# Transposing row tiles two matmuls earlier, and moving one projection between the last value products

## The chip, the cores and the metric

The kernel runs on one core of one Trainium2 chip. The metric is the device time of one execution in microseconds, taken as the median of several. A profiled execution gives a trace with a start and a recorded end for every instruction. In the views of the profile PE is the tensor engine, PEld its weight loads, DVE VectorE, ACT ScalarE, POOL GpSimd and SP SyncE; a q behind a name marks the start of a transfer on that engine's queue, and L302 is line 302 of the kernel.

## The reference

```python
def reference(A_x, A_k_cache, A_v_cache, A_wq, A_wo, B_x, B_w_gate, B_w_up, B_w_down):
    x = A_x                                   # (1, 2048, 640)
    xn = _layernorm(x, axis=-1)
    s = _A_ref(xn, A_k_cache, A_v_cache, A_wq, A_wo)   # attention, 32 heads of 192, last 512 keys
    g = _silu(_B_ref(xn, B_w_gate, B_w_up, B_w_down))  # (sigmoid(xn@Wg) * (xn@Wu)) @ Wd
    return x + s * g
```

All arrays are bfloat16. There is no causal mask: every row meets the same 512 keys.

## The kernel before

Two places matter. In the **prologue** the first 512 rows are taken as four row tiles of 128. A tile is centred on VectorE (tile 0 in part on ScalarE), turned on the tensor engine by five transposes (`turn_pe`), copied by ScalarE in two parts out of PSUM (the memory that the matmuls write), and then serves as weights for five gate and five up matmuls of 512 columns (`tile_half`, with half 0 for gate and 1 for up; `c0`, `c1` choose some of the five chunks).

```python
        def turn_pe(t, c0=0, c1=NCD, k=3):
            pT = bank[k][:, t % 2, 0:NCD * H2].bitcast(BF16).rearrange("p (c n) -> p c n", c=NCD)
            for c in range(c0, c1):
                nc.tensor.transpose(pT[:, c, :], xn_t[t][:, c * P:(c + 1) * P], ident[:])
            for d0, d1 in ((c0, c1),) if c1 - c0 < NCD else ((0, 3), (3, NCD)):
                nc.scalar.activation(xcT[:, d0:d1, t * P:(t + 1) * P], pT[:, d0:d1, :], AF.Copy)
        ...
        for t in range(1, TQ):
            if t > 1:
                tile_half(t, 0, t % 3, 0)
            tile_half(t, 0, t % 3, 1, 0, 3)
            if t + 1 < TQ:
                turn_pe(t + 1)
            tile_half(t, 0, t % 3, 1, 3)
            if t == 1:
                tile_gated(0, 0, 0)
            tile_gated(t, 0, t % 3)
```

At the **end**, `values` (one head's product with V) and `project` (one row tile through Wo) run as two half passes each, which add into the same PSUM bank. Between the halves VectorE copies two numbers per partition out of the bank into `seen`. Only then may the second half start, so the copy is a marker that the first half is complete. `flow` puts other passes between the halves:

```python
    def values(u, h, k):
        ...
        for turn in range(2):
            ...                                # 16 matmuls of 193 columns, in pairs of 64 rows
            if turn == 0:
                nc.vector.tensor_copy(seen[:, DJ, :], bank[k][:, :, 0])
                yield
        ...                                    # reciprocal, then o_st = o4 * rden, both on VectorE

    def flow(jobs):                            # a0 b0 a1 c0 b1 d0 c1 ... : halves 0 and 1
        before = None
        for j in jobs:
            next(j)
            if before is not None:
                next(before)
            before = j
        next(before)

    order = (2, 3, 0, 1)
    ...
    flow([values(u + 1, h, order[h]) for h in range(4)]
         + [project(u - 1, 0, order[0], nc.scalar, nc.gpsimd)])
    for q in range(1, 4):
        next(project(u - 1, q, order[q], nc.scalar, nc.gpsimd, False))
    for q in range(4):
        next(project(u, q, order[q], nc.sync, nc.vector, False))
    last_rows()
```

The softmax here doesn't subtract the row's maximum and nothing guards it: scores larger than these inputs give would overflow.

## Time and profile before

| | before |
|---|---|
| median of the first three runs | 922.3 us |
| span of the profiled run (that run's time) | 919.8 us (921.55 us) |
| tensor engine busy | 99% of the span |
| last up matmul of tile 1 to first gate matmul of tile 2, start to start | 0.530 us (0.216 where nothing waits) |
| the same, tile 2 to tile 3 | 0.530 us |
| last score matmul to first 128-row projection ("the end stretch") | 8.139 us |

A matmul's recorded end is modelled (a 512-column matmul is recorded with 0.38 us and the next starts after 0.216), so distances between starts are what to read. Of the matmuls with gate, up and down weights and the first queries about one in fifty is missing from the trace (19 of 924); where one is, a distance looks twice as long and a count is one short.

### The profile page before, as it was taken

How to read it: one execution, taken by the hardware profiler on the slowest of the kernel's cores; microseconds unless marked ns; L12 is line 12 of the kernel's file. 1: busy time of each engine (PE TensorE's matmuls, PEld its weight loads, DVE VectorE, ACT ScalarE, POOL GpSimd, SP SyncE). 2: the span in 40 equal slices, each digit the busy share in tenths (PEclk: the TensorE clock that was granted, in tenths of full speed). 3: DMA queues.
4: the chain of work that ended last, by engine and by line, in shares of the span. 5: the costliest groups of instructions: out<-in, count | busy, mean ns of one | idle time of the engine just before them, and what ended most of it. 6: DMA issues, size and time to landing. Idle time of an engine off the chain costs nothing.

```text
span 919.8 us, 24974 instructions
## 1 busy us (share of the span) xinstructions
PE 913.4 (99%) x11314; PEld 622.9 (68%) x11333; DVE 492.9 (54%) x987; ACT 303.1 (33%) x334; POOL 126.7 (14%) x147
## 2 busy tenths in 40 slices
PE   9999999999999999999999999999999999999998
PEld 4445455466868686867676777777776767686885
DVE  6452522444646464646555555545564646464667
ACT  4222222255142424242333333242424151515150
POOL 2000100011002000200020011001100111055813
PEclk9999999999999999999999999999999999999999
DMA  9820330115434434342425162525251615246435
GB/s 319 165 44 1 89 87 1 43 62 88 80 61 110 83 59 81 94 98 44 97 83 109 36 105 79 113 32 108 65 110 44 113 61 88 62 96 142 89 72 138
DMA packets 173642, 79.35 MB, mean 86 GB/s; under 512 B 149952, under 2 KB 169616, under 8 KB 173536
## 3 DMA queue, kind: packets, MB, share of 16 engines
q1 hardware_dynamic: 166944, 58.47, 32.1%
q0 software_dynamic: 5040, 17.89, 6.7%
q8 instruction: 88, 1.44, 0.7%
q10 hardware_dynamic: 1552, 1.39, 0.5%
q14 instruction: 18, 0.15, 0.1%
HBM read 39.45 MB, written 2.62 MB: 46 GB/s over the span
## 4 chain that ended last, share of the span: by engine, by line
PE 99%; DMA 0%; DVE 0%; issue 0%; ACT 0%; DVEq 0%
PE bank L530 22%; PE bank L456 21%; PE bank L478 19%; PE bank L438 18%; PE bank L260 8%; PE bank L272 6%; PE bank L302 3%; PE bank L404 1%; DMA wg_sb<-in_B_w_gate_dram 0%; PE bank L563 0%; DVE o_sb L508 0%; DVE gate L513 0%; ACT xnT L246 0%; PE bank L244 0%; DVEq L665 0%
## 5 line engine op out<-in xcount | busy, mean ns | idle before, releaser
L442 ACT ACTIVATE E<-bank 128x1024 bf16<-128x1024 f32 x256 | 255.4, 1022 | 456.4 <-PE bank L438 456.3
L456 PE MATMUL bank<-xnT,wq_sb 64*128 64x512 bf16 x1800 | 226.4, 376 | 0.0
L530 PE MATMUL bank<-wo_sb,oT 64*128 64x320 bf16 x2688 | 205.2, 296 | 0.0
L438 PE MATMUL bank<-qT,kT 64*128 64x512 bf16 x1536 | 200.7, 376 | 0.0
L478 PE MATMUL bank<-vbuf,E 64*128 64x193 bf16 x4096 | 195.3, 243 | 0.0
L478 PEld LDWEIGHTS <-E 64*128 64x128 bf16 x4096 | 178.8, 94 | 10.2 <-issue 0.3
L530 PEld LDWEIGHTS <-oT 64*128 64x128 bf16 (+1 forms) x2892 | 163.3, 94 | 30.6 <-issue 0.3
L463 DVE CAST qT<-bank 128x1024 bf16<-128x1024 f32 x90 | 110.2, 1225 | 128.5 <-PE bank L456 128.5
L456 PEld LDWEIGHTS <-wq_sb 64*128 64x128 bf16 x1800 | 106.1, 100 | 87.0 <-issue 0.4
L438 PEld LDWEIGHTS <-kT 64*128 64x128 bf16 x1536 | 88.1, 94 | 73.5
L491 DVE TENSOR_TENSOR o_st<-bank,rden 128x768 bf16<-128x768 f32 x128 | 122.5, 957 | 4.4
L545 DVE TENSOR_TENSOR acc<-bank,acc 128x640 f32<-128x640 f32 x96 | 79.1, 824 | 20.1 <-PE bank L530 20.1
L118 POOL DMA_DIRECT2D vbuf<-in_A_v_cache_dram x28 | 21.1, 755 | 310.2 <-PE bank L478 307.3
L461 DVE COPY seen<-bank 128x2 f32<-128x2 f32 x90 | 14.3, 159 | 79.1 <-PE bank L456 79.1
L490 DVE RECIPROCAL rden<-bank 128x4 f32<-128x4 f32 x128 | 23.4, 183 | 60.6 <-PE bank L478 59.5
L272 PE MATMUL bank<-wd_sb,hT 128*128 128x128 bf16 (+1 forms) x377 | 52.4, 298 | 0.4
L272 PEld LDWEIGHTS <-hT 128*128 128x128 bf16 x384 | 29.7, 98 | 23.1
L260 PE MATMUL bank<-xnT,wu_sb 128*128 128x512 bf16 x177 | 44.6, 379 | 0.2
L260 PE MATMUL bank<-xnT,wg_sb 128*128 128x512 bf16 x176 | 44.5, 379 | 0.2
L266 DVE TENSOR_TENSOR hT<-bank,sig 128x512 bf16<-128x512 f32 x36 | 24.8, 690 | 37.1 <-ACT sig L263 37.1
L263 ACT ACTIVATE sig<-bank 128x512 bf16<-128x512 f32 x36 | 21.5, 597 | 55.8 <-PE bank L260 52.7
L110 POOL COPY k_perm<-k_st 128x768 bf16<-128x768 bf16 x32 | 25.5, 827 | 76.6 <-DMA k_st<-in_A_k_cache_dram 76.6
(52 smaller groups left out, 379.5 us busy)
## 6 DMA issues: line engine op xcount, KB each, us to landing
wo_sb<-in_A_wo_dram SPq DMA_DIRECT2D x7, 960.0 KB, 5.6
wq_sb<-in_A_wq_dram POOLq DMA_DIRECT2D x7, 960.0 KB, 6.0
k_st<-in_A_k_cache_dram POOLq DMA_DIRECT2D x14, 384.0 KB, 5.9
vbuf<-in_A_v_cache_dram POOLq DMA_DIRECT2D x28, 192.0 KB, 3.8
row<-in_A_x_dram SPq DMA_DIRECT2D x16, 160.0 KB, 2.4
oT<-o_st SPq DMA_TRANSPOSE x128, 3.2
x_sb<-in_A_x_dram SPq DMA_DIRECT2D x3, 640.0 KB, 9.5
wd_sb<-in_B_w_down_dram SPq DMA_DIRECT2D x1, 1920.0 KB, 13.8
```

The lines of the kernel that those rows point to most:

```text
L110: nc.gpsimd.tensor_copy(kp[:, pr, :, :, i * H2:(i + 1) * H2], kst[:, i, :, :].rearrange("p c (i j) -> p c j i", j=DJ),)
L260: nc.tensor.matmul(bank[k][:, half, 0:r1 - r0], lhsT=w[:, c, f * P:(f + 1) * P], rhs=xnT[:, b, c, r0:r1], start=(c == 0), stop=(c == NCD - 1))
L272: nc.tensor.matmul(wide(k)[:, d0:d1], lhsT=hT[b][:, f, q * P:(q + 1) * P], rhs=wd_sb[:, f, d0:d1], start=(f == 0), stop=(f == NF - 1))
L302: nc.tensor.matmul(bank[k][:, half, :], lhsT=xcT[:, c, t * P:(t + 1) * P], rhs=w[:, c, fg * FT:(fg + 1) * FT], start=(c == 0), stop=(c == ...
L438: nc.tensor.matmul(bank[k][:, i, :], lhsT=kT[r, pr, j, c * P:(c + 1) * P], rhs=q[r, pr * DJ + j, :], start=(j == 0), stop=(j == DJ - 1))
L442: nc.scalar.activation(E[u, pr][:, c, :, :], bank[k][:], AF.Exp, scale=scale_qk)
L456: nc.tensor.matmul(bank[k][:, half, :], lhsT=wq[r, c, col:col + DJ * (P - 1) + 1:DJ], rhs=xnT[r, b, c, :], start=(c == 0 and not second), ...
L463: nc.vector.tensor_copy(qT[u][:, 2 * m:2 * m + 2, :], bank[k][:])
L478: nc.tensor.matmul(o4[:, q, 0:DH + 1], lhsT=e[r, c, h % 2, q * P:(q + 1) * P], rhs=vbuf[r, h, c, 0:DH + 1], start=(turn == 0 and qq == 0 a ...
L491: nc.vector.tensor_tensor(o_st[u][:, :, h * DH:(h + 1) * DH], o4[:, :, 0:DH], rden[:].to_broadcast([P, TQ, DH]), ALU.mult)
L530: nc.tensor.matmul(res[:, half, :], lhsT=oT[u][r, cc, q * P:(q + 1) * P], rhs=wo[r, cc, half * HD:(half + 1) * HD], start=(turn == 0 and c ...
L545: nc.vector.tensor_tensor(cols(acc[:, t, :]), res, cols(acc[:, t, :]), ALU.add)
```

## The change

Its intent is to take away standing time of the tensor engine: in the prologue by putting four up matmuls instead of two behind the transposes, so that ScalarE's copy is done when the gate matmuls need it; at the end by putting a longer pass between the halves of the first value product.

```diff
-            tile_half(t, 0, t % 3, 1, 0, 3)
+            tile_half(t, 0, t % 3, 1, 0, 1)
             if t + 1 < TQ:
                 turn_pe(t + 1)
-            tile_half(t, 0, t % 3, 1, 3)
+            tile_half(t, 0, t % 3, 1, 1)
@@
-    flow([values(u + 1, h, order[h]) for h in range(4)]
-         + [project(u - 1, 0, order[0], nc.scalar, nc.gpsimd)])
+    flow([values(u + 1, 0, 2), project(u - 1, 0, 3, nc.scalar, nc.gpsimd),
+          values(u + 1, 1, 0), values(u + 1, 2, 1), values(u + 1, 3, 2)])
```

## The prediction

> **What bounds the kernel now.** I read the page first. Its span, 919.8 us, is of the profiled execution; the timed median is 922.3 us, 2.5 us more, and I carry that difference over unchanged.
>
> ```profile
> PE 913.4 (99%) x11314; PEld 622.9 (68%) x11333; DVE 492.9 (54%) x987; ACT 303.1 (33%) x334; POOL 126.7 (14%) x147
> ...
> PE 99%; DMA 0%; DVE 0%; issue 0%; ACT 0%; DVEq 0%
> ```
>
> The tensor engine is busy 99% of the span and is 99% of the chain of waits that ended last. The change moves instructions and removes none, so it can win only time in which the tensor engine stood still. I therefore looked next for such time in the view of waits, and then in the timeline of the two stretches that the diff touches. In the table of waits almost nothing lasts on this engine: its weight loads wait for ScalarE's copies into xnT five times, 2.0 us in total, all in the prologue.
>
> A matmul's end is modelled, so I count from start to start. In steady stretches five 512-column matmuls start every 1.08 us (13.64, then 14.73, then 15.81), which is 0.216 us each. The timeline of the prologue, with start and length in us, then shows this:
>
> ```profile
> 8.98 0.52 DVE L233 TENSOR_SCALAR xn<-x_sb,mv 128x384 bf16<-128x384 bf16 x2
> ...
> 9.86 0.44 PE L244 MATMUL bank<-ident,xn 128*128 128x128 bf16 x5
> ...
> 10.33 0.76 ACT L246 ACTIVATE xnT<-bank 128x384 bf16<-128x384 bf16 x2 [2.86 <-PE bank L244]
> 10.35 0.38 PE L302 MATMUL bank<-wu_sb,xnT 128*128 128x512 bf16 x1
> ...
> 10.88 1.25 PE L302 MATMUL bank<-wg_sb,xnT 128*128 128x512 bf16 x5 [0.15 <-ACT xnT L246]
> ...
> 12.62 0.44 PE L244 MATMUL bank<-ident,xn 128*128 128x128 bf16 x5
> 12.89 0.59 PE L302 MATMUL bank<-wu_sb,xnT 128*128 128x512 bf16 x2
> 13.10 0.77 ACT L246 ACTIVATE xnT<-bank 128x384 bf16<-128x384 bf16 x2 [0.84 <-PE bank L244]
> ...
> 13.64 1.25 PE L302 MATMUL bank<-wg_sb,xnT 128*128 128x512 bf16 x5 [0.15 <-ACT xnT L246]
> ```
>
> The last up matmul of tile 1 starts at 10.35. The next, the first gate matmul of tile 2, could start at 10.35 + 0.216 = 10.566, but starts at 10.88: 0.314 us are lost, twice the 0.15 that the view prints, because that counts from the modelled end. The cause is a chain: five transposes, ScalarE copies them out (first copy 10.33 to 10.825), and only then does the gate matmul have its weights. Only two up matmuls, 0.43 us, lie behind the transposes to cover about 0.75 us. The same happens for tile 3, whose last up matmul starts at 13.11: 13.64 - 13.327 = 0.314.
>
> The timeline of the end:
>
> ```profile
> 889.92 5.69 PE L478 MATMUL bank<-vbuf,E 64*128 64x193 bf16 x128
> ...
> 891.02 0.96 DVE L491 TENSOR_TENSOR o_st<-bank,rden 128x768 bf16<-128x768 f32 x1
> 891.89 0.46 DVE L485 COPY seen<-bank 128x2 f32<-128x2 f32 x2
> ...
> 895.43 0.99 PE L530 MATMUL bank<-wo_last,oT 64*128 64x320 bf16 x12
> ...
> 896.24 0.85 PE L478 MATMUL bank<-vbuf,E 64*128 64x193 bf16 x16
> 896.74 0.15 DVE L536 COPY seen<-bank 128x2 f32<-128x2 f32 x1
> 896.83 0.77 PEld L530 LDWEIGHTS <-oT 64*128 64x128 bf16 x12
> 896.94 12.51 PE L530 MATMUL bank<-wo_last,oT 64*128 64x320 bf16 x96
> ```
>
> In the chain view a value product (32 matmuls) takes 1.33 us and a projection (24) 1.63 us, so a half pass is 0.667 or 0.815 us. The eight value passes from 889.92 should end at 895.25, but the projection starts at 895.43: 0.18 us lost. It lies at 891.92, where the second half of the first value product waits for VectorE's small "seen" copy (891.89 to 892.04), which stands behind the 0.96 us eviction of the unit before. A second loss, 0.03 us, is at 896.94: 896.24 + 0.667 is 896.91, but the projection's second half waits for its own seen copy, which ends at 896.89.
>
> **What the Trainium skill says.** "TensorE: Matmul & The Clock Gate", section "Back-to-back issue gap", gives an isolated gap of N/2.4 + 2.5 ns: 216 ns for 512 columns and 136 for 320. The trace agrees (0.216; 1.63 us for 12 row-group pairs is 0.136). "Perfetto Trace Analysis", section "Tensor Engine Instruction (MATMUL, LD_WEIGHTS)", says that a matmul's profiled end is estimated from its size; this trace agrees, as matmuls of 0.38 us start 0.216 apart, so I use starts alone. "TensorEngine Tiling (Array Packing)", section "Key Properties", says that changing the tiling mode drains the engine. The trace has one such change near the edit: from 64-row to 128-row matmuls the next start is at 897.86 where 896.94 + 0.815 = 897.75 was due, 0.11 us. The change keeps this switch, behind another product.
>
> **Part one, the prologue.** The transposes of tiles 2 and 3 now stand behind one up matmul in place of three. No instruction is added. Four up matmuls, 0.864 us, then cover the copy. Worked out for tile 2: the transposes start two matmuls earlier, at 9.86 - 0.43 = 9.42; the copy keeps its distance of 0.48 us and starts at 9.90, and its first part (0.49 us) ends at 10.39; a release took 0.055 us before (10.825 to 10.88), so the gate matmul is free at 10.45 and due at 10.566. Slack 0.12 us, wait gone, 0.314 us won, and another 0.009 us because the first matmul behind the old wait took 0.225 us to the next. For tile 3 everything stands 0.32 us earlier as well: transposes at 11.86, copy 12.34 to 12.83 (ScalarE's two sigmoids also move up and end near 11.8), gate free at 12.89 and due at 13.005. Another 0.32 us. **Sum: 0.65 us won.**
>
> The earlier transposes need VectorE's centred rows sooner. For tile 2 the two parts end near 9.30 and 9.50; transpose 1 is due at 9.42 and transpose 4 at 9.59. Each part has its own wait in the built program, so with the same 0.055 us release the slack is 0.06 and 0.04 us: just enough. Tile 3's rows are ready at 11.15, well before 11.86.
>
> **Part two, the end.** The first half of one projection moves between the first two value products. Pass by pass, from the first value half at 890.585: the projection's half is due at 891.25, where its bank is free (the last exponential ends at 891.16, as before); it ends at 892.07, and the next value half is released at 892.10 by the same seen copy. The loss falls from 0.18 to 0.03 us. But now the fourth value product closes the sequence, with one pass (0.667 us) between its halves where it had two. Its seen copy stands in VectorE's order behind the second product's eviction. That product's second half runs 894.91 to 895.58; its reciprocal starts at 895.80 (0.22 us behind, as before), its eviction 896.02 to 896.98, the seen copy 896.89 to 897.04 (such copies start 0.08 us before the eviction's recorded end), and the matmul is released at 897.09. It was due at 896.91. A new wait of 0.18 us. Totals: before 0.18 + 0.03 = 0.21, after 0.03 + 0.18 = 0.21. **Sum: nothing**, within about 0.1.
>
> The early output row (VectorE, GpSimd, DMA) leaves about 3.8 us sooner, but it isn't the last row. The last unit's transposes wait for a free oT buffer until the other three projections have read theirs, near 902.9, so a later last eviction (near 899.4 in place of 898.3) doesn't delay them.
>
> **The total.** 922.3 - 0.65 + 0.0 = 921.65, say 921.7 us, 0.07% less.
>
> **Rivals.** First, the wait moves from ScalarE to VectorE: with 0.04 us of slack, a row of x that lands 0.3 us later than in this trace (DMA is saturated there, at some 350 GB/s) would cost up to 0.26 us of part one. For it: the first ten microseconds hang on transfers. Against it: the three times lie within 0.4 us of each other. Time: 921.9 or 922.0. Second, the tensor engine, now 0.65 us early, meets weights or transposed rows that have not landed, and gives the gain back: 922.3. Against it: no later wait of this engine for a DMA is in the list; in the trace the up weights next needed (at 16.24) land at 12.7, and the transposed rows needed at about 32.6 land at 30.5. Third, the new wait at the end is bigger than 0.18 us, because one more VectorE instruction slips in front of the seen copy: each 0.1 us there is 0.1 us of time, so 921.9 at 0.4 us. Or it doesn't arise and the end also wins its 0.18 us: 921.5.
>
> **Range and chances.** The removable standing time in both places is 0.63 + 0.21 us, so below about 921.4 there is nothing to be had except scatter; the repeats differ by up to 0.4 us. If most of part one is lost and the end loses 0.2, it is 922.4. I take 921.2 to 922.4. Two per cent is 18 us, over twenty times all that moves, so faster and slower get half a per cent each.
>
> **What would show it.** In the changed kernel's timeline the first gate matmul of tiles 2 and 3 should start 0.216 us behind the last up matmul, near 10.57 and 13.0, and the table of waits should lose these two waits for ScalarE. The transposes' loads should start without waiting for xn. At the end the value half behind the projection's half should wait 0.03 us or less, and the very last value half about 0.2 us. I would be wrong if the gate matmuls still wait, if a wait for xn over 0.1 us appears in front of the transposes, or if the last value half starts at once or waits over 0.4 us.

## The result, and the profile after

The changed kernel took 921.28 us in the median (921.04 to 921.51, four runs), the kernel before 922.2 us over four runs. The ratio is 0.9991 with a 95% interval of 0.9973 to 1.0008, so the times alone do not tell the two apart. A ratio here is the mean time of one kernel's runs over that of the other's of the same rounds, so not quite the ratio of the medians quoted.

The page of the changed kernel has the same picture as before, with 0.6 us less busy tensor engine:

```profile
PE 912.8 (99%) x11314; PEld 622.7 (68%) x11333; DVE 492.5 (54%) x987; ACT 303.3 (33%) x334; POOL 126.7 (14%) x147
```

The number drops although no matmul was removed: where nothing waits, the recorded matmuls overlap, so the first part of a wait behind one of them is counted as busy. Of the 0.62 us, 0.35 lie in the prologue between the first up matmul and the next rows' first gate matmul, where the two waits were; the other 0.27 lie before that, in the start-up, which differs from run to run (below). The view of waits, in us in total, number and longest, of the kernel before:

```profile
PEld L302 <- ACT xnT L246: 2.0, 5, 0.6
```

and of the changed kernel:

```profile
PEld L302 <- ACT xnT L246: 1.2, 5, 0.4
```

The group still counts five waits, but two of them are now weight loads that start ahead of time and hold nothing up. In the same view the waits of the matmuls themselves, `PE bank L302 <- ACT xnT L246`, go from two of 0.15 us to a single one of 0.28 us, at 5.46 in the start-up. That the loads are ahead of time is to be seen only in the timeline of the changed kernel's prologue (start, length, engine):

```profile
9.53 0.44 PE L244 MATMUL bank<-ident,xn 128*128 128x128 bf16 x5
...
9.81 1.03 PE L302 MATMUL bank<-wu_sb,xnT 128*128 128x512 bf16 x3
10.01 0.77 ACT L246 ACTIVATE xnT<-bank 128x384 bf16<-128x384 bf16 x2 [2.43 <-PE bank L244]
...
10.55 1.08 PEld L302 LDWEIGHTS <-xnT 128*128 128x128 bf16 x6 [0.21 <-ACT xnT L246]
...
10.67 1.24 PE L302 MATMUL bank<-wg_sb,xnT 128*128 128x512 bf16 x5
...
12.25 1.03 PE L302 MATMUL bank<-wu_sb,xnT 128*128 128x512 bf16 x4
...
12.99 1.30 PEld L302 LDWEIGHTS <-xnT 128*128 128x128 bf16 x7 [0.21 <-ACT xnT L246]
13.11 1.24 PE L302 MATMUL bank<-wg_sb,xnT 128*128 128x512 bf16 x5
```

Four up matmuls from 9.81 (one record of the four is missing) put the next start at 9.81 + 4 x 0.216 = 10.67, and there the gate matmul starts; likewise 12.25 + 0.864 = 13.11. Neither gate matmul's line carries an idle time, and the weight loads with one, at 10.55 and 12.99, start 0.12 us before the matmuls they serve. ScalarE's first copy ran from 10.01 to 10.50, well inside.

The timeline of the changed kernel's end:

```profile
890.71 0.99 PE L530 MATMUL bank<-wo_last,oT 64*128 64x320 bf16 x12
891.35 0.15 DVE L485 COPY seen<-bank 128x2 f32<-128x2 f32 x1
...
891.55 1.51 PE L478 MATMUL bank<-vbuf,E 64*128 64x193 bf16 x32
...
893.70 3.69 PE L478 MATMUL bank<-vbuf,E 64*128 64x193 bf16 x80
...
895.47 0.96 DVE L491 TENSOR_TENSOR o_st<-bank,rden 128x768 bf16<-128x768 f32 x1
896.34 0.15 DVE L485 COPY seen<-bank 128x2 f32<-128x2 f32 x1
896.55 0.61 PEld L478 LDWEIGHTS <-E 64*128 64x128 bf16 x15 [0.17 <-issue]
...
897.32 2.02 PEld L530 LDWEIGHTS <-oT 128*128 128x128 bf16 x16 [0.16 <-issue]
```

The projection's half pass ends at 890.711 + 0.815 = 891.526, and the value half behind it starts at 891.555: 0.03 us lost where 0.18 were lost before. The five passes from 893.70 (80 matmuls) should end at 897.03. Four of them do take their 2.67 us, to 896.37, but the fifth starts only at 896.55, 0.055 us after the seen copy, which came behind the 0.96 us eviction that started at 895.47. That is a new wait of 0.18 us. The end stretch takes 8.139 us again, to the nanosecond.

**How to compare when the times scatter by more than the effect.** The start of the first up matmul of tile 0 moves between 8.09 and 8.97 us from run to run in the fourteen traces, whatever the kernel. From there to the first gate matmul of the next 512 rows, and in the end stretch, the traces repeat to within 0.005 us. So I cut the span there:

| kernel | profiled run, us | first up matmul at | from it to the next rows' first gate matmul | end stretch | time less start |
|---|---|---|---|---|---|
| before | 921.55 | 8.13 | 24.949 | 8.139 | 913.42 |
| after | 921.04 | 8.24 | 24.300 | 8.139 | 912.81 |

The change won 0.649 us in the prologue and 0.000 at the end. (The last column differs by 0.61 us only, because the time of the run exceeds the span of the trace by 1.77 us before and 1.81 us after.)

The expectations of the first eight runs count the end from the first value matmul (889.92 in the trace of before) and not, as this column does, from the last score matmul 0.196 us earlier: their 7.94 us is the 8.139 here, and their 7.73 us would be 7.93.

### The profile page after: what moved, and what is told of

Its sections match the earlier page's. It is cut to its first block, busy times and chain, and to the rows that moved or that the text cites. A ratio compares the mean times of both kernels' runs of the same rounds, so it can differ in the third digit from the quotient of the medians.

```text
span 919.2 us, 24975 instructions
## 1 busy us (share of the span) xinstructions
PE 912.8 (99%) x11314; PEld 622.7 (68%) x11333; DVE 492.5 (54%) x987; ACT 303.3 (33%) x334; POOL 126.7 (14%) x147
## 4 chain that ended last, share of the span: by engine, by line
PE 99%; DVE 0%; DMA 0%; issue 0%; ACT 0%; DVEq 0%
PE bank L530 22%; PE bank L456 21%; PE bank L478 19%; PE bank L438 18%; PE bank L260 8%; PE bank L272 6%; PE bank L302 3%; PE bank L404 1%; PE bank L563 0%; DMA x_sb<-in_A_x_dram 0%; DVE o_sb L508 0%; DVE gate L513 0%; PE bank L244 0%; ACT xn L236 0%; DVE st L202 0%
```

## The experiments

Twelve kernels ran, each correct, with five rounds, in three sets of four; each set shared its runs of the kernel before. The last column of the table is the profiled run's time less the start of its first up matmul, as above.

| run | median, us | ratio to before, 95% interval | prologue piece | end stretch | time less start |
|---|---|---|---|---|---|
| e1_null | 921.72 | 0.9993, 0.9980 to 1.0006 | 24.950 | 8.141 | 913.78 |
| e2_prologue_only | 921.28 | 0.9992, 0.9980 to 1.0004 | 24.300 | 8.139 | 912.77 |
| e3_end_only | 921.91 | 0.9999, 0.9986 to 1.0011 | 24.947 | 8.143 | 913.42 |
| e4_both | 921.63 | 0.9991, 0.9979 to 1.0003 | 24.300 | 8.141 | 912.80 |
| e5_two_three | 921.39 | 0.9996, 0.9984 to 1.0008 | 24.536 | 8.138 | 913.04 |
| e6_none_five | 921.01 | 0.9994, 0.9982 to 1.0006 | 24.300 | 8.138 | 912.81 |
| e7_seen_on_act | 922.75 | 1.0005, 0.9993 to 1.0017 | 24.300 | 9.398 | 914.09 |
| e8_two_projections | 920.96 | 0.9987, 0.9975 to 0.9999 | 24.300 | 9.620 (7.99 without the moved 1.63) | 912.62 |
| e9_old_order_on_act | 921.26 | 0.9994, 0.9982 to 1.0007 | 24.300 | 7.939 | 912.58 |
| e10_act_row_by_sync | 921.46 | 0.9995, 0.9981 to 1.0008 | 24.300 | 7.939 | 912.61 |
| e11_two_again | 921.13 | 0.9995, 0.9983 to 1.0008 | 24.300 | 9.625 (7.99) | 912.63 |
| e12_both_again | 921.68 | 0.9997, 0.9985 to 1.0010 | 24.300 | 8.140 | 912.82 |

My theory before the runs: the whole gain is the prologue's 0.63 us, because the copy is covered; the end gains nothing, because a wait for a seen copy went and another came. The rivals: part of the 0.9 us between the medians comes from the end; any earlier turning would do; the wait at the end belongs to the copy itself and not to what stands in front of it.

**e1_null.** The kernel before with one comment line added.

> The kernel before with one comment line added; it measures the noise. Every theory expects a ratio of 1.000 to the kernel before; how far the interval and the median stray from it (I expect up to 0.0004, some 0.4 us) is what the other runs of this set have to be read against. In the trace the first gate matmuls of row tiles 2 and 3 start 0.53 us behind the last up matmul, as before, and the end (first value half of the last unit's predecessor pass to the first 128-row projection, 889.92 to 897.86 in the trace of before) takes 7.94 us.

Its ratio is 0.9993, nearly as far from 1 as the 0.9991 of the change itself. Its profiled run lost a further 0.35 us in the middle, at one projection (start to start 0.539 us) that waited for VectorE while that engine took 1.98 us over one sum; I did not look for its cause. So no ratio in this table, except perhaps that of e8, says anything by itself, and the pieces must.

**e2_prologue_only.** The first hunk of the diff alone.

> The first hunk of the change alone. Main theory (the prologue wins about 0.63 us, the end nothing): the whole gain, 0.63 us, ratio 0.9993, both gate matmuls of tiles 2 and 3 at 0.216 us behind the last up matmul. Rival (the early output row or the new order at the end wins part of the 0.9 us that the medians differ by): only 0.4 us or less here, ratio 0.9996 or more. The end still takes 7.94 us.

The prologue piece is 24.300 us, that of the full change, and the time less start is 912.77 against 912.81. The first rival falls. This profiled run also began late, with its first up matmul at 8.97. The timeline of this run's start shows why:

```profile
5.47 0.61 PE L302 MATMUL bank<-wg_sb,xnT 128*128 128x512 bf16 x1 [0.16 <-ACT xnT L246]
5.87 0.42 PE L244 MATMUL bank<-ident,xn 128*128 128x128 bf16 x2
6.08 1.05 PE L302 MATMUL bank<-wg_sb,xnT 128*128 128x512 bf16 x2
```

The same instructions in the trace of after:

```profile
5.46 0.39 PE L302 MATMUL bank<-wg_sb,xnT 128*128 128x512 bf16 x1 [0.28 <-ACT xnT L246]
5.69 0.27 PE L244 MATMUL bank<-ident,xn 128*128 128x128 bf16 x2
5.80 0.59 PE L302 MATMUL bank<-wg_sb,xnT 128*128 128x512 bf16 x2
```

A 512-column matmul is recorded with 0.61 us instead of 0.39, and two of them with 1.05 instead of 0.59: until about 7 us this run's tensor engine went at about half its pace. Every trace begins so: the warm-up matmuls of 256 columns start 0.213 us apart in all fourteen, and only in after, e5 and e10 do the last of them reach 0.109 us. What differs is how long the slow pace lasts, and the clock that the views print does not show it (1.00 from 4 to 8 us in e2). Slow starts that make a run late by half a microsecond and more are in e7 and e8 too, and e1, with the old order, has a shorter one (its first gate matmul at 5.56 takes 0.59 us, its first up matmul starts at 8.56). All instructions that the change moves come later, so these starts are not its doing.

**e3_end_only.** The second hunk alone.

> The second hunk alone. Main theory: no gain, ratio 1.000, the end takes 7.94 us as before, with a wait of 0.03 us where there was 0.18 and a new one of 0.16 to 0.18 us in front of the last value half. Rival (the end is worth something of its own): 0.2 to 0.3 us, ratio 0.9997, and the end takes 7.7 us. The two gate matmuls keep their 0.53 us.

The end stretch is 8.143 us, and the time less start is that of the kernel before, 913.42. The last value half waits here too, in front of the same instruction. The end is worth nothing.

**e4_both**, the changed kernel again.

> The changed kernel again with one comment line added, beside the halves. Main theory: the same as the prologue alone, ratio 0.9993 (0.6 us). Rival (0.9 us gain in the medians is real and part comes from the end): ratio 0.9990 and clearly below the prologue alone.

24.300 and 8.141 us; 912.80. The same as the prologue alone. By the medians it is 0.35 us slower than e2, which shows what the medians are worth.

**e5_two_three.** Two up matmuls ahead, three behind.

```diff
-            tile_half(t, 0, t % 3, 1, 0, 3)
+            tile_half(t, 0, t % 3, 1, 0, 2)
             if t + 1 < TQ:
                 turn_pe(t + 1)
-            tile_half(t, 0, t % 3, 1, 3)
+            tile_half(t, 0, t % 3, 1, 2)
```

> Prologue of the change with two up matmuls ahead of the transposes and three behind (before three and two, after one and four), end as before. Main theory (what counts is the cover behind the transposes: the gate matmul is free 1.026 us after the first transpose, and due 0.28 us plus 0.216 us for each up matmul behind): with three behind it is due at 0.928, so a wait of 0.10 us is left at each of tiles 2 and 3, the start-to-start distance is 0.31 to 0.32 us, and the gain is 0.63 - 0.2 = 0.42 us. Rival (any move of the transposes ahead removes the wait, because ScalarE had been held by something else): distance 0.216 us and the full 0.63 us.

The timeline around tile 2 in this run:

```profile
10.29 0.59 PE L302 MATMUL bank<-wu_sb,xnT 128*128 128x512 bf16 x2
10.82 1.25 PE L302 MATMUL bank<-wg_sb,xnT 128*128 128x512 bf16 x5
```

The last up matmul starts at 10.29 + 0.216 = 10.50 and the gate matmul at 10.82, 0.315 us later: a wait of 0.10 us is left, and the same at tile 3 (0.314). The piece is 24.536 us, a gain of 0.413 us where 0.42 was expected; 0.02 us of the piece went to a weight transfer that landed at 8.89, so that an up matmul of tile 0 due at 8.91 started at 8.93. The wait follows the amount of cover, matmul by matmul, so the rival that any earlier turning would do falls. The view marks no idle time on that gate line: the wait is hidden there, and only the starts show it.

**e6_none_five.** All five up matmuls behind the transposes.

```diff
-            tile_half(t, 0, t % 3, 1, 0, 3)
             if t + 1 < TQ:
                 turn_pe(t + 1)
-            tile_half(t, 0, t % 3, 1, 3)
+            tile_half(t, 0, t % 3, 1, 0)
```

> Transposes ahead of all five up matmuls, end as before. Main theory: no wait for ScalarE is left (0.216 us), but the transposes of tile 2 are now due about 0.05 us after, or up to 0.15 us before, VectorE's centred rows are ready, so a wait for xn of 0 to 0.2 us appears there, depending on when the row of x lands; tile 3 has none; gain 0.43 to 0.63 us. Rival (VectorE is comfortably ahead): no wait at all, 0.63 us, the same as one and four.

24.300 us, the full gain and no more: once the copy is covered, further cover is worth nothing. The wait for VectorE that I thought possible did not hold up a matmul. In this trace the first centred part was complete at 9.18, and the weight load of the first transpose waited for it, to 9.236 in place of 9.117; but the transpose itself started at 9.33, on time. Its tensor engine had begun 0.12 us later than in the trace of before, so with an early start and the same arrival of x, it could still come; no run here shows that.

**e7_seen_on_act.** The changed kernel with the seen copies of the last flow made by ScalarE.

```diff
+    seen_act = acc_pool.tile([P, 2], F32, name="seen_act")
+    late = []
@@ values; project likewise
-                nc.vector.tensor_copy(seen[:, DJ, :], bank[k][:, :, 0])
+                if late:
+                    nc.scalar.activation(seen_act[:], bank[k][:, :, 0], AF.Copy)
+                else:
+                    nc.vector.tensor_copy(seen[:, DJ, :], bank[k][:, :, 0])
@@
+    late.append(True)
     flow([values(u + 1, 0, 2), project(u - 1, 0, 3, nc.scalar, nc.gpsimd),
```

> The changed kernel, but the seen copies of the last flow are made by ScalarE, which is idle there, in place of VectorE. Main theory (the standing time of the end is the seen copy queued behind VectorE's 0.96 us eviction): both waits, 0.03 and 0.18 us, vanish; the end takes 7.73 us in place of 7.94, and the time is 0.2 us below the changed kernel, ratio to before about 0.9991. Rival (the wait is the time that a copy of PSUM takes to come back, whoever makes it): the end stays at 7.9 us or gets longer, because a ScalarE copy takes no less.

A miss: the end stretch grew to 9.398 us. The timeline of this run:

```profile
893.74 0.17 ACT L488 ACTIVATE seen_act<-bank 128x2 f32<-128x2 f32 x1 [1.15 <-PE bank L480]
...
895.48 1.53 POOL L518 TENSOR_TENSOR gate<-o_sb,acc 128x640 bf16<-128x640 f32 x1 [19.27 <-DVE o_sb L513]
...
897.04 0.36 ACTq L519 DMA_DIRECT2D out_dram<-gate  x1
897.53 0.38 ACT L488 ACTIVATE seen_act<-bank 128x2 f32<-128x2 f32 x2 [3.62 <-DVE o_st L496]
897.75 1.34 PE L480 MATMUL bank<-vbuf,E 64*128 64x193 bf16 x28 [1.28 <-ACT seen_act L488]
```

The copies themselves are quick (0.17 us). But ScalarE also starts the transfer of the projected row, and in its order that start stands in front of the last two seen copies. It waits for GpSimd's 1.53 us sum (to 897.01), and behind it the copies run at 897.53. From 894.29 three value passes end at 896.29; the fourth starts at 897.75, 1.46 us late. 9.398 - 1.46 = 7.94, so but for this the stretch would have been what I expected (7.73 us in the count of that text, 7.93 here). That reading was tested in e10.

**e8_two_projections.** A second projection between the halves of the last value product.

```diff
           values(u + 1, 1, 0), values(u + 1, 2, 1), values(u + 1, 3, 2),
+          project(u - 1, 1, 3, nc.scalar, nc.gpsimd)])
-    for q in range(1, 4):
+    for q in range(2, 4):
```

> The changed kernel with a second projection of the same rows put between the halves of the last value product, so that the last value half has two passes behind its first half again. Main theory: the new wait of 0.18 us goes, and one of 0.03 us appears in front of that projection's own second half, as in the kernel before; 0.15 us less than the changed kernel, ratio to before about 0.9991 to 0.9992. Rival (the wait is tied to the end of the sequence, whatever stands there): the closing half waits 0.15 us or more again, no gain.

Without the 1.63 us of projection that moved into it, the stretch is 7.99 us, 0.15 less than the changed kernel, as expected, and the ratio of 0.9987 is the only one whose interval does not hold 1. Its repeat, e11, gave 0.9995, so I do not rest anything on that. The wait is not tied to the end of the sequence: it comes with a cover of one pass, and with two it is gone.

**e9_old_order_on_act.** The prologue of the change, the old order at the end, seen copies by ScalarE.

> The prologue of the change, the old order at the end, and ScalarE makes the seen copies of the last flow. In this order ScalarE has no output transfer to start before the last seen copy. Main theory (the standing time is the seen copy queued behind something in the order of its engine, not the order of the passes): both waits of the old order, 0.18 and 0.03 us, vanish; from the last score matmul to the first 128-row projection it takes 8.139 - 0.21 = 7.93 us, and the time is 0.2 us below the changed kernel. Rival (a ScalarE copy is too slow to come back in one pass of 0.667 us, and that made the last run of this kind slow): a wait stays, 8.1 us or more.

7.939 us, 0.20 less than before and after: both waits of the old order are gone, and a copy by ScalarE, 0.17 us, comes back within one pass, against the rival. There ScalarE's transfer start stands behind the last seen copy.

**e10_act_row_by_sync.** e7 with the projected row sent by another queue.

```diff
-    flow([values(u + 1, 0, 2), project(u - 1, 0, 3, nc.scalar, nc.gpsimd),
+    flow([values(u + 1, 0, 2), project(u - 1, 0, 3, nc.sync, nc.gpsimd),
```

> As the run with the seen copies on ScalarE that was 1.3 us slower at the end than expected, but the one early output row is sent by SyncE's queue in place of ScalarE's. Main theory (there the copies were stuck behind ScalarE's start of that row's transfer, which waits for GpSimd's 1.54 us sum): the wait of 1.44 us is gone, the stretch from the last score matmul to the first 128-row projection takes 7.93 us as in the old order, in place of 9.398. Rival (ScalarE needs long for these copies for another reason): the stretch stays above 8.14 us.

The timeline of this run, where the last two seen copies now follow their passes at once:

```profile
893.57 3.51 PE L480 MATMUL bank<-vbuf,E 64*128 64x193 bf16 x80
...
895.83 0.17 ACT L488 ACTIVATE seen_act<-bank 128x2 f32<-128x2 f32 x1 [1.16 <-PE bank L480]
...
897.01 0.72 PE L535 MATMUL bank<-wo_last,oT 128*128 128x320 bf16 x4
```

Eighty matmuls from 893.57 are due to end at 896.90, and the 128-row projection follows 0.11 us later. No wait is left; 7.939 us again. What e7 lost was the place of the transfer start in ScalarE's order. It also shows that the order of the passes does not matter once the copies are not queued: e9 and e10 have different orders and the same stretch.

**e11_two_again and e12_both_again**, on the chip of e9 and e10.

> The version with two projections once more, beside the changed kernel and the two ScalarE versions on one chip: the stretch 9.620 us again (it holds 1.63 us of projection that was outside it before, so 7.99 against 8.139), 0.15 us below the changed kernel, and 0.06 us above the two ScalarE versions, which the times can't tell apart.

> The changed kernel once more as the yardstick of this set: the stretch 8.139 us, ratio to the kernel before 0.9993 by the main theory (0.63 us), and 0.15 to 0.2 us above the other three.

Both repeat their pieces to 0.005 us. By the pieces e9 and e10 are 0.85 us below the kernel before (0.649 + 0.200), e11 0.80 and the changed kernel 0.65. The medians of this set, 921.26, 921.46, 921.13 and 921.68, put the changed kernel last as expected, but the intervals of the ratios overlap, and the changed kernel's median even equals that of the kernel before in its set (921.68). So a version that beats both is shown in the trace and not in the times.

## Why the prediction was right

- **The prologue, 0.65 us.** Measured 0.649 us in every trace with the first hunk. The gate matmuls start 0.216 us behind the last up matmul. ScalarE's copy came 0.48 us after the first transpose, as assumed. e5 confirms the sum by its parts: one up matmul less behind the transposes leaves 0.10 us per tile.
- **The slack of VectorE's rows, 0.04 to 0.06 us.** No matmul waited; 24.300 us in nine further traces, though in e4 and e11 a transpose's load did start up to 0.07 us late for its rows. The rival did not happen, and that is in part luck. The first centred part was complete between 0.27 us (e2) and 1.38 us (e5) behind the first up matmul, and the changed kernel's first transpose is due 1.295 us behind it. Rows as late as those of e5, which ran with two up matmuls ahead, would by my estimate have cost the changed kernel about 0.14 us (1.38 + 0.055 for the release, less 1.295).
- **The end, 0.21 us before and 0.21 after.** The first value half waits 0.03 us, the last 0.18 us, the stretch is unchanged at 8.139 us. The predicted new wait (released 0.18 us late, behind the second product's eviction) was the one seen. e3 shows it with the second hunk alone.
- **The total.** 921.28 us lies in 921.2 to 922.4, though 0.4 us below the point. The term at fault is the 2.5 us between span and time. I took it from the median of 922.3 and the span of one run; that run itself took 921.55 us, so the difference is 1.8 us in it (and 921.04 - 919.2 = 1.8 us after). The other 0.7 us is by how much the median of before lay above its profiled run, which is scatter. The traces show one place where scatter arises, the first 9 us (first up matmul from 8.09 to 8.97), and e1 a second, 0.35 us in the middle; whether the untraced runs of before lost their time there is not shown. So that the total fell inside the range says little: 0.65 us is less than the scatter, and 921.28 lies below the 921.4 under which the prediction itself saw nothing but scatter. What bears the prediction out is the pieces.
- **The rivals for weights or transposed rows not landed** did not occur: the pieces behind the prologue are the same in both kernels (129.860 us from the next rows' first gate matmul to the first query matmul, and from there 726.785 and 726.786 us to the last score matmul).

## What to carry to other kernels

Here, with the tensor engine busy 99% of the span, a reordering was worth the standing time it removed (0.649 us predicted as 0.65), and that was found in distances between starts rather than in recorded idle times. The wait for a small marker copy was a matter of what stood in front of it in its engine's order, be it a long eviction (0.18 us) or the start of a transfer that waits (1.46 us in e7); moving the passes around it moved the wait, and moving the copy to an engine with nothing in front of it removed it (e9, e10). Where the effect is below the scatter of the times, cut the trace at fixed instructions and compare the pieces.

## What the Trainium skill lacked or had wrong

- "TensorEngine Tiling (Array Packing)", "Key Properties", says that a change of tiling mode drains the engine, but gives no time. Here the step from 64-row to 128-row matmuls took 0.11 us more than the plain distance (0.248 us from the start of the last pair, where 0.136 was due), and the one from 128-row to 64-row about 0.10 us (0.312 where 0.216 was due).
- "TensorE: Matmul & The Clock Gate", "Back-to-back issue gap", gives 131 ns per matmul for sustained pairs of weight load and 512-column matmul, and says that the isolated formula over-counts there. In this kernel such pairs start every 0.216 us, which is the isolated formula's value.
- "Perfetto Trace Analysis", "DVE / Act Engine Instruction (TENSOR_ADD, Activation, etc)", shows that a semaphore's update still has to spread behind the recorded end, without a time. Here a waiting matmul started 0.05 to 0.06 us after the recorded end of the ScalarE or VectorE instruction that released it (10.825 to 10.880, 896.49 to 896.545).
- The same page, "Tensor Engine Instruction (MATMUL, LD_WEIGHTS)", calls ScalarE strictly first in, first out, but has no example of what that costs when the start of a transfer stands in the same order. Here one that waited for its data held back ScalarE's later copies and cost 1.46 us in e7, and nothing once another queue sent the row in e10.
